# Layer norm's reciprocal standard deviation: square root on ScalarE and reciprocal on VectorE, or add and power on GpSimd

## The chip, the cores and the metric

The kernel runs on one core of one Trainium2 chip. The metric is the device time of one execution in microseconds (us). One step of the norm, done 30 times on small tiles (128 partitions x 2), is moved from ScalarE and VectorE to GpSimd; the big work, 7424 matmuls, is the same in both kernels.

Engine names in the profile: PE is TensorE's matmul, PEld its weight load, DVE is VectorE, ACT is ScalarE, POOL is GpSimd. SBUF is the on-chip memory that tiles lie in; PSUM is the one that matmuls write to. A hole is a stretch in which TensorE is idle. The granted clock of TensorE is given as a share of full speed.

## The reference, cut to what matters

Two layers. Each is a norm, a sliding-window attention (`_A_ref`, 8 dilated positions), a norm, and a gated feed-forward (`_B_ref`).

```python
def _layernorm(x, axis=-1, eps=1e-5):
    m = jnp.mean(x, axis=axis, keepdims=True)
    v = jnp.var(x, axis=axis, keepdims=True)
    return (x - m) / jnp.sqrt(v + eps)

def _B_ref(x, w1, w3, w2):
    gate = jnp.einsum("bsd,df->bsf", x, w1)
    up = jnp.einsum("bsd,df->bsf", x, w3)
    h = _silu(gate) * up
    return jnp.einsum("bsf,fd->bsd", h, w2)

x = x + _A_ref(_layernorm(x), A_wqkv, A_wo)     # x is 1 x 2048 x 1024
x = x + _B_ref(_layernorm(x), B_w1, B_w3, B_w2) # 1024 -> 3584 -> 1024
# ... and the same two lines again
```

## The kernel before: what the change and the argument touch

The program is a list of eight feed-forward units, 0 to 7: two layers times four chunks of 512 tokens. Beneath the matmuls of a unit VectorE works on the attention of the *next* unit: multiplications `pr` (scores) and `tm` (values), each with two operands in SBUF, and their sums. At two places of the unit, at tile 19 and tile 27 of 28, half a norm of the next unit is inserted. That half runs with the same raised priority as the products `hT` that TensorE waits for.

```python
def ln_half(key, c, r):                      # half a norm: two token tiles
    with hp():                               # raised priority
        ...
        for i in range(2):
            n = c * TPC + 2 * r + i
            for hh in range(2):
                nc.vector.bn_stats(st[:, i, hh, :], x_sb[:, n, hh * 512:(hh + 1) * 512])
            nc.vector.bn_aggr(mv[:, i, :], st[:, i, :, :])
        nc.scalar.activation(sd[:], mv[:, :, 1], ACTF.Sqrt, bias=epst[:])
        nc.vector.reciprocal(rstd[:], sd[:])
        for i in range(2):
            j = 2 * r + i
            xn = xnp.tile([P, D], BF16, name="xn")
            nc.vector.tensor_scalar(xn[:], x_sb[:, c * TPC + j, :], mv[:, i, 0:1], rstd[:, i:i + 1],
                                    op0=ALU.subtract, op1=ALU.mult)
            nc.sync.dma_start_transpose(out=xnT[:, :, j * P:(j + 1) * P], in_=xn[:])

def b_stage(l, c, inserts):                  # one unit
    for (f0, f1) in fsplits:                 # (0, 16), then (16, 28)
        ... # for each tile f, after what `inserts` has for it:
                pg = ...                     # 8 matmuls: gate
                pu = ...                     # 8 matmuls: up
                with hp():
                    nc.scalar.activation(sg[:], pg[:], ACTF.Silu)
                    nc.vector.tensor_tensor(hT[:, g0 + fi - f0, :], sg[:], pu[:], op=ALU.mult)
        for hh in range(2):
            for j in range(TPC):
                acc = bank("acc")
                for f in range(f0, f1):      # second product; needs hT of all f
                    nc.tensor.matmul(acc[:], lhsT=hT[:, f - f0, j * P:(j + 1) * P], rhs=...,
                                     start=(f == f0), stop=(f == f1 - 1))
                ...                          # x_sb += acc

# in the loop over the units; n and c2 are of the next unit:
ins = {17: [O(l2, n)], 19: [O(l2, n + 1), lambda: ln_half(("B", l2, c2), c2, 0)],
       25: [O(l2, n + 2)], 27: [O(l2, n + 3), lambda: ln_half(("B", l2, c2), c2, 1)]}
```

I call the second product after tiles 0 to 15 "acc A" (128 matmuls) and the one after tiles 16 to 27 "acc B" (96 matmuls). The twelfth matmul of acc B needs the `hT` of tile 27, the last one. "First half" and "second half" are the calls of `ln_half` at tile 19 and tile 27.

## Time and profile before

| | before |
|---|---|
| median of 3 runs, us | 1636.41 (1635.89 to 1637.51) |
| span of the profiled run, us | 1635.4 |
| granted TensorE clock, mean | 0.998 |
| ScalarE table loads | 59 |

The busy table of the page (busy us, share of the span, number of instructions) says which engine is the limit:

```profile
PE 1616.1 (99%) x7472; PEld 800.2 (49%) x7472; DVE 1152.4 (70%) x1961; ACT 340.5 (21%) x530; POOL 1.9 (0%) x12
```

TensorE is busy for all but about 19 us: 5.2 of these are in the first 13.9 us, the start, and 3.5 come after the last matmul. The list of waits of the kernel before (who waited on which line for whom: total us, times, longest us) has nearly all of the rest:

```profile
PEld L327 <- DVE hT L314: 9.0, 8, 2.6
...
PE pg L305 <- DMA xnT<-xn: 4.9, 1, 4.9
PE acc L327 <- DVE hT L314: 4.7, 3, 2.1
```

So the last `hT` of a stage is already late in three of the sixteen acc stages, 4.7 us together. TensorE nowhere waits for ScalarE's square root; VectorE's reciprocal does, five times, 2.5 us in all.

What the change will take away stands among the groups of instructions of ScalarE (count, busy us, mean ns, idle us before them). Line 128 is the square root; 40 more table loads belong to Silu, Exp and the start:

```profile
L128 ACT ACT_TABLE_LOAD x19 | 24.4, 1283 | 1.4 <-DVE mv L125 1.2
L128 ACT ACTIVATE sd<-mv,epst 128x2 f32<-128x2 f32 x30 | 8.7, 295 | 127.8 <-DVE mv L125 127.7
```

A load takes 1283 ns, which is what the Trainium skill, "ScalarE: Activation LUTs", What ACT_TABLE_LOAD costs, states. The page adds a drain of about 1380 ns to each switch; this trace shows none. At 1464 us the square root ends at 1464.69, a load runs from 1464.71 to 1465.99, and Silu starts at 1466.00: 1.31 us from end to start.

Last, the timeline at the end of unit 2 (start us, duration us, engine, line, what, and in brackets the idle time before it and its releaser):

```profile
705.25 21.13 PE L327 MATMUL acc<-w2t,hT 128*128 128x512 bf16 x96
...
705.92 0.20 DVE L125 BATCH_NORM_AGGREGATE mv<-st 128x2 f32<-128x12 f32 x1
706.03 1.17 DVE L228 TENSOR_TENSOR pr<-qT,kT 128x2048 bf16<-128x2048 bf16 x1
706.15 0.29 ACT L128 ACTIVATE sd<-mv,epst 128x2 f32<-128x2 f32 x1 [0.53 <-DVE mv L125]
707.12 0.68 DVE L314 TENSOR_TENSOR hT<-sg,pu 128x512 bf16<-128x512 bf16 x1
707.72 0.15 DVE L129 RECIPROCAL rstd<-sd 128x2 f32<-128x2 f32 x1
...
708.38 0.54 DVE L133 TENSOR_SCALAR xn<-x_sb,mv,rstd 128x1024 bf16<-128x1024 bf16 x1
```

Acc B starts at 705.25 us, and its 96 matmuls run in one piece. VectorE goes from one instruction to the next without a pause: the square root (706.15 to 706.44) hides under `pr`, and the last `hT` ends at 707.80, about when the twelfth matmul needs it.

### The profile page before, as it was taken

To read this page: it belongs to the slowest core of one execution; us is meant where nothing else is said; L and a number is where in the kernel's file an instruction comes from. 1 tells how busy PE (TensorE), PEld (TensorE's weight loads), DVE (VectorE), ACT (ScalarE), POOL (GpSimd) and SP (SyncE) were. 2 spreads that over 40 slices of the span, in tenths; PEclk is the share of its full clock that TensorE was granted. 3 is DMA by queue.
4 is the path that set the end of the run, shared out by engine and by line. 5 is a ranking of instruction groups with operands and counts; after the bars stand their busy time and mean duration, and the time that the engine had idled before them with its cause. 6 is when DMAs were issued, how large, how long until landed. Compare 5 with 4: busy or idle time off the path is not lost.

```text
span 1635.4 us, 18944 instructions
## 1 busy us (share of the span) xinstructions
PE 1616.1 (99%) x7472; PEld 800.2 (49%) x7472; DVE 1152.4 (70%) x1961; ACT 340.5 (21%) x530; POOL 1.9 (0%) x12
## 2 busy tenths in 40 slices
PE   8999899999999999999999999999999999999999
PEld 5666444444444644446444554445544444444444
DVE  4899999999999781897728977299652992332212
ACT  3333311203021320223202232022320211121110
POOL 0000000000000000000000000000000000000000
PEclk9999999999999999999999999999999999999999
DMA  9943746557546774367743686438753574256440
GB/s 297 280 132 102 220 158 195 159 151 209 183 131 180 240 235 150 106 193 245 221 142 104 199 259 200 142 104 249 255 178 119 129 232 155 90 143 205 155 129 26
DMA packets 337113, 286.32 MB, mean 175 GB/s; under 512 B 69632, under 2 KB 319488, under 8 KB 336896
## 3 DMA queue, kind: packets, MB, share of 16 engines
q1 hardware_dynamic: 337024, 285.11, 57.2%
q8 instruction: 58, 0.95, 0.2%
q14 instruction: 31, 0.25, 0.0%
HBM read 239.99 MB, written 29.36 MB: 165 GB/s over the span
## 4 chain that ended last, share of the span: by engine, by line
PE 67%; DVE 29%; issue 3%; DMA 1%; ACT 0%; DVEq 0%; ACTq 0%
PE acc L327 21%; PE pg L305 15%; PE pu L309 15%; PE ps L202 13%; DVE pr L228 5%; DVE tm L273 4%; PE po L283 3%; DVE hT L314 3%; DVE tm L174 3%; DVE pr L174 2%; DVE x_sb L287 1%; DVE st L124 1%; DVE tm L175 1%; DVE pr L175 1%; DVE L L235 1%
## 5 line engine op out<-in xcount | busy, mean ns | idle before, releaser
L305 PE MATMUL pg<-xnT,w1t 128*128 128x512 bf16 x1792 | 424.7, 380 | 4.9 <-DMA xnT<-xn 4.9
L309 PE MATMUL pu<-xnT,w3t 128*128 128x512 bf16 x1792 | 423.7, 379 | 0.0
L327 PE MATMUL acc<-w2t,hT 128*128 128x512 bf16 x1792 | 390.8, 379 | 5.1 <-DVE hT L314 4.7
L202 PE MATMUL ps<-xnT,wqkv 128*128 128x512 bf16 x1536 | 334.3, 380 | 1.8 <-ACT xnT L163 1.1
L313 ACT ACTIVATE sg<-pg 128x512 bf16<-128x512 f32 x224 | 133.4, 597 | 843.2 <-PE pg L305 831.4
L314 DVE TENSOR_TENSOR hT<-sg,pu 128x512 bf16<-128x512 bf16 x224 | 152.1, 679 | 212.2 <-PE pu L309 210.7
L305 PEld LDWEIGHTS <-w1t 128*128 128x128 bf16 x1792 | 175.5, 98 | 217.0 <-issue 6.6
L327 PEld LDWEIGHTS <-hT 128*128 128x128 bf16 x1792 | 174.8, 98 | 218.5 <-DVE hT L314 9.0
L309 PEld LDWEIGHTS <-w3t 128*128 128x128 bf16 x1792 | 175.5, 98 | 212.0 <-issue 1.0
L202 PEld LDWEIGHTS <-wqkv 128*128 128x128 bf16 x1536 | 220.5, 144 | 114.6 <-issue 3.9
L332 DVE TENSOR_TENSOR x_sb<-x_sb,acc 128x512 bf16<-128x512 bf16 x128 | 87.0, 680 | 162.2 <-PE acc L327 162.2
L228 DVE TENSOR_TENSOR pr<-qT,kT 128x2048 bf16<-128x2048 bf16 x128 | 153.1, 1210 | 51.6 <-issue 32.1
L273 DVE TENSOR_TENSOR tm<-At,vT 128x2048 bf16<-128x2048 bf16 x128 | 151.7, 1213 | 0.3
L204 ACT CAST sgt<-ps 128x512 bf16<-128x512 f32 x192 | 108.7, 588 | 184.6 <-PE ps L202 151.7
L283 PE MATMUL po<-wo,oT 128*128 128x512 bf16 x512 | 115.4, 379 | 0.0
L124 DVE BATCH_NORM_STATS2 st<-x_sb 128x6 f32<-128x512 bf16 x120 | 79.9, 681 | 18.0 <-DMA x_sb<-in_A_x_dram 17.3
L174 DVE TENSOR_TENSOR pr<-pr 128x1024 bf16<-128x1024 bf16 x128 | 85.6, 680 | 0.0
L174 DVE TENSOR_TENSOR tm<-tm 128x1024 bf16<-128x1024 bf16 x128 | 84.4, 681 | 0.0
L283 PEld LDWEIGHTS <-oT 128*128 128x128 bf16 x512 | 50.0, 98 | 60.4
L287 DVE TENSOR_TENSOR x_sb<-x_sb,po 128x512 bf16<-128x512 bf16 x64 | 43.2, 677 | 15.4 <-PE po L283 15.4
L175 DVE TENSOR_TENSOR pr<-pr 128x512 bf16<-128x512 bf16 x128 | 51.8, 415 | 0.2
L175 DVE TENSOR_TENSOR tm<-tm 128x512 bf16<-128x512 bf16 x128 | 50.3, 415 | 0.1
(169 smaller groups left out, 428.7 us busy)
## 6 DMA issues: line engine op xcount, KB each, us to landing
w1t<-in_B_w_dram SPq DMA_DIRECT2D x56, 1024.0 KB, 5.4
w3t<-in_B_w_dram SPq DMA_DIRECT2D x56, 1024.0 KB, 7.2
w2t<-in_B_w_dram SPq DMA_DIRECT2D x48, 1024.0 KB, 5.4
wqkv<-in_A_wqkv_dram SPq DMA_DIRECT2D x28, 1024.0 KB, 6.6
w2t<-in_B_w_dram SPq DMA_DIRECT2D x16, 512.0 KB, 5.1
qkv_d_0_158<-sgt SPq DMA_DIRECT2D x16, 256.0 KB, 5.3
qkv_d_1_159<-sgt SPq DMA_DIRECT2D x16, 256.0 KB, 4.4
qT<-qkv_d_0_158 SPq DMA_DIRECT2D x8, 512.0 KB, 4.0
```

The costliest lines, as they stand in the source:

```text
L174: nc.vector.tensor_tensor(buf[:, 0:4, :], buf[:, 0:4, :], buf[:, 4:8, :], op=ALU.add)
L175: nc.vector.tensor_tensor(buf[:, 0:2, :], buf[:, 0:2, :], buf[:, 2:4, :], op=ALU.add)
L202: nc.tensor.matmul(ps[:], lhsT=ws[kk // KH][:, kk % KH, t::KT], rhs=xnT[:, kk, :], start=(kk == 0), stop=(kk == KT - 1))
L204: nc.scalar.copy(sgt[:, t - t0, :], ps[:])
L228: nc.vector.tensor_tensor(pr[:], qT[:], kT[:, :, k0:k0 + TCH], op=ALU.mult)
L273: nc.vector.tensor_tensor(tm[:], At[:], win, op=ALU.mult)
L283: nc.tensor.matmul(ps[:], lhsT=oT[:, t, j * P:(j + 1) * P], rhs=wo[:, t, hh * 512:(hh + 1) * 512], start=(t == 0), stop=(t == KT - 1))
L305: nc.tensor.matmul(pg[:], lhsT=w1t[:, kk, fi * P:(fi + 1) * P], rhs=xnT[:, kk, :], start=(kk == 0), stop=(kk == KT - 1))
L309: nc.tensor.matmul(pu[:], lhsT=w3t[:, kk, fi * P:(fi + 1) * P], rhs=xnT[:, kk, :], start=(kk == 0), stop=(kk == KT - 1))
L313: nc.scalar.activation(sg[:], pg[:], ACTF.Silu)
L314: nc.vector.tensor_tensor(hT[:, g0 + fi - f0, :], sg[:], pu[:], op=ALU.mult)
L327: nc.tensor.matmul(acc[:], lhsT=hT[:, f - f0, j * P:(j + 1) * P], rhs=w2ts[(f - f0) // 8][:, (f - f0) % 8, :], start=(f == f0), stop=(f == ...
```

## The change

ScalarE spends 24.4 us on loading the square root's tables, and more on loading those of Silu and Exp again, because the three alternate. The intent is to have no square root there at all: GpSimd, which is idle, adds epsilon and raises the sum to the power of minus one half, and VectorE is rid of the reciprocal.

```diff
+    mhalf = const.tile([P, 2], FP32, name="mhalf")
+    nc.gpsimd.memset(mhalf[:], -0.5)
 ...
             sd = small.tile([P, 2], FP32, name="sd")
             rstd = small.tile([P, 2], FP32, name="rstd")
-            nc.scalar.activation(sd[:], mv[:, :, 1], ACTF.Sqrt, bias=epst[:])
-            nc.vector.reciprocal(rstd[:], sd[:])
+            nc.gpsimd.tensor_tensor(sd[:], mv[:, :, 1], epst[:].to_broadcast([P, 2]), op=ALU.add)
+            nc.gpsimd.tensor_tensor(rstd[:], sd[:], mhalf[:], op=ALU.pow)
```

## The prediction

> **What bounds the kernel.** TensorE. The busy table has PE at 1616.1 of 1635.4 us, clock granted at 0.998. In the timeline eight 128x512 matmuls take 1.73 us, so the 7424 large matmuls need about 1603 us (estimate). The list of waits and the timeline leave these holes in PE: the start (13.9 us, a norm routine that the change does not touch), about 6.7 us at 196 to 206 us (first feed-forward stage, waiting for the transposed norm), 2.3, 2.0 and 0.9 us at 261, 345 and 424 us (second product waiting for hT), 0.7 us at 187 us. So at most 12 us (0.8%) could be won.
>
> **What goes.** On ScalarE: 30 square roots (295 ns each, 8.7 us) and their 19 table loads (1283 ns each, 24.4 us). The Trainium skill, "ScalarE: Activation LUTs", What ACT_TABLE_LOAD costs, gives the same 1283 ns. ScalarE is busy 21%; none of the five PE holes was ended by it, the late hT being held by VectorE's queue. On VectorE: 30 reciprocals, 158 ns, 4.7 us of 1152. So nearly all of the saving is off the critical path.
>
> **What comes.** 30 adds and 30 powers of 128x2 on GpSimd, in series with two more hand-overs. The trace has no such instruction; a memset of 128x1 takes 0.10 us, an affine select 0.28. I estimate 0.2 us for an add and 0.5 us for a power, 0.8 to 1.2 us from the statistics to rstd including hand-overs, against 0.57 us in the tight case at 1464 us.
>
> **What moves.** TensorE's order is unchanged. VectorE's is not: the scheduler now puts the apply (xn) ahead of the last hT of a feed-forward stage. Before: aggregate, pr, hT, reciprocal, xn. After, in units 1 to 4 (of 0 to 7): aggregate, pr, xn, hT; in units 0 and 5 two xn. VectorE works in order, so hT now waits for GpSimd. There is no slack there: in unit 1 hT ended at 507.26 us and the twelfth matmul of acc needs it at about 507.25. And the Trainium skill, "SBUF — State Buffer", Who interferes with whom, says a VectorE instruction with two SBUF inputs and a GpSimd instruction reading SBUF exclude each other: the add, released while pr (1.17 us) runs, would start only after pr. No run shows that yet. Then hT is late by xn (0.46) plus 0.8, about 1.3 us, five times, plus half a us more in unit 5: 7 us; unit 0 about +1.4. The hole at 196 to 206 us: as before. VectorE's freed 4.7 us may take 1 us off the holes at 261 and 424.
>
> **Sum.** 1636.4 + 7 + 1.4 - 1 is about 1644 us; 1635 to 1657 should hold it 8 times in 10. Same within 2%: 0.93; slower 0.06; faster 0.01.
>
> **What would show it.** Table loads fall from 59 to 29 and ScalarE's busy time by 47 us, without a shorter span. PE waits "acc <- hT" at five or six stage ends, 1 to 2 us each; VectorE waits about 1 us for rstd before xn. GpSimd's add starting as pr ends shows the port claim; starting within pr refutes it.
>
> **What would make it wrong.** A power that takes 2 to 3 us (then each stage end loses 3 us or more, 1655 to 1660); GpSimd not blocked by pr (then only 0.5 us a unit, about 1639); a VectorE order that shrinks the other holes (then equal or 3 us faster).

## The result, and the profile after

| | before | after |
|---|---|---|
| median, us (4 runs each, same rounds) | 1636.72 | 1660.41 (1658.9 to 1661.61) |
| ratio | | 1.0143, 95% interval 1.0128 to 1.0159 |
| span of the profiled run, us | 1635.4 | 1658.6 |
| granted clock, mean | 0.998 | 0.990 |
| ScalarE busy, us / table loads | 340.5 / 59 | 296.6 / 29 |

Here and below a ratio is the mean time of one kernel's fast runs over the mean of the other's fast runs of the same rounds, so it is not quite the ratio of the medians.

The kernel became 1.4% slower. That is within 2%, as expected, but above the upper end of the range (1657). The busy table after:

```profile
PE 1626.2 (98%) x7472; PEld 803.1 (48%) x7472; DVE 1154.0 (70%) x1931; ACT 296.6 (18%) x470; POOL 40.2 (2%) x73
```

ScalarE lost 43.9 us of work. TensorE, with the same number of matmuls, was busy 10 us longer, and 13 us more of its time lies idle. The waits after:

```profile
DVE xn L135 <- POOL rstd L131: 21.0, 27, 1.1
PE acc L329 <- DVE hT L316: 18.4, 8, 2.9
...
PE pg L307 <- DMA xnT<-xn: 4.3, 1, 4.3
```

VectorE now waits 27 times for GpSimd, and TensorE's wait for `hT` rose from 4.7 to 18.4 us. The new groups of GpSimd:

```profile
L131 POOL TENSOR_TENSOR rstd<-sd,mhalf 128x2 f32<-128x2 f32 x30 | 21.9, 734 | 2.0
L130 POOL TENSOR_TENSOR sd<-mv,epst 128x2 f32<-128x2 f32 x30 | 16.4, 551 | 1445.6 <-DVE mv L127 1445.6
```

The add's mean of 551 ns mixes mainly two kinds, 0.20 us and about 1.06 us. All twelve of 1.06 us ran beside a `pr` or `tm`, and each ended 0.05 or 0.06 us after it. The timeline has one of each: the first line is from the first norm of the feed-forward, beside a VectorE instruction with one input in PSUM; the others are from unit 2, first half (676 to 679 us) and second half (712 us on).

```profile
187.52 0.20 POOL L130 TENSOR_TENSOR sd<-mv,epst 128x2 f32<-128x2 f32 x1 [120.67 <-DVE mv L127]
...
676.16 1.17 DVE L275 TENSOR_TENSOR tm<-At,vT 128x2048 bf16<-128x2048 bf16 x1
676.33 1.06 POOL L130 TENSOR_TENSOR sd<-mv,epst 128x2 f32<-128x2 f32 x1 [139.70 <-DVE mv L127]
677.47 0.69 POOL L131 TENSOR_TENSOR rstd<-sd,mhalf 128x2 f32<-128x2 f32 x1
678.19 1.00 DVE L135 TENSOR_SCALAR xn<-x_sb,mv,rstd 128x1024 bf16<-128x1024 bf16 x2 [0.86 <-POOL rstd L131]
...
712.23 2.54 PE L329 MATMUL acc<-w2t,hT 128*128 128x512 bf16 x11
713.75 0.20 DVE L127 BATCH_NORM_AGGREGATE mv<-st 128x2 f32<-128x12 f32 x1
713.87 1.17 DVE L230 TENSOR_TENSOR pr<-qT,kT 128x2048 bf16<-128x2048 bf16 x1
714.03 1.06 POOL L130 TENSOR_TENSOR sd<-mv,epst 128x2 f32<-128x2 f32 x1 [35.87 <-DVE mv L127]
715.17 0.69 POOL L131 TENSOR_TENSOR rstd<-sd,mhalf 128x2 f32<-128x2 f32 x1
715.89 0.55 DVE L135 TENSOR_SCALAR xn<-x_sb,mv,rstd 128x1024 bf16<-128x1024 bf16 x1 [0.86 <-POOL rstd L131]
716.35 0.68 DVE L316 TENSOR_TENSOR hT<-sg,pu 128x512 bf16<-128x512 bf16 x1
717.09 20.21 PE L329 MATMUL acc<-w2t,hT 128*128 128x512 bf16 x85 [2.32 <-DVE hT L316]
```

Read it in four steps.

1. The add is on record from 714.03 but ends at 715.09, 0.05 us after `pr` (713.87 to 715.04). Elsewhere it takes 0.20 us. Then comes the power, 0.69 us, and VectorE, which works in order, stands still for 0.86 us.
2. `xn` now stands ahead of `hT` in VectorE's order, 0.46 us from its start to the start of `hT`.
3. The same 0.86 us were lost once already, in the first half at 678 us. VectorE never has a pause afterwards in which to make them good: the aggregate of the second half comes 1.52 us after the start of acc B (713.75 - 712.23), where it came 0.67 us after it before (705.92 - 705.25). The difference is 0.85 us.
4. The sum, 0.86 + 0.86 + 0.46 = 2.18 us, is the size of the hole, 2.32 us. After the hole 85 matmuls take 20.21 us. In kernels with a short hole the same 85 take 18.52 us (below).

For step 4, look at the hole of unit 1 (510.0 to 512.79 us) in windows. The columns are window, us, then busy us of PE, PEld, DVE, ACT, POOL with the number of instructions, then the granted clock, the DMA share and GB/s:

```profile
512.50:514.00 1.50, 1.21 (x3) 0.43 (x4) 1.50 (x4) 0.00 (x0) 0.00 (x0) 0.50 0.48 92
514.00:516.00 2.00, 2.00 (x6) 0.73 (x5) 2.00 (x5) 0.00 (x0) 0.00 (x0) 0.53 0.90 152
516.00:518.00 2.00, 2.00 (x11) 0.90 (x10) 2.00 (x4) 0.00 (x0) 0.00 (x0) 1.00 1.02 381
```

The clock is 0.50 for about three microseconds after the hole, and a matmul takes twice as long in it: 6 began in the second window, 11 in the third. PE reads as fully busy in both, so the busy row does not show it.

The ledger, from the timeline of TensorE, each stage from its start to the start of the next, in us:

| stage | before | after | difference |
|---|---|---|---|
| acc A of unit 0 | 29.91 | 31.81 | +1.90 |
| acc B of unit 0 | 22.75 | 23.77 | +1.02 |
| acc A of unit 1 | 28.55 | 28.30 | -0.25 |
| acc B of units 1, 2, 3, 4, 5 | 20.96 each | 25.20, 24.90, 24.91, 24.91, 25.36 | +20.48 |
| sum | | | +23.15 |

The spans differ by 23.2 us, so this is all of it. Acc B of unit 6, where no norm follows, is 20.72 us in both.

### The profile page after: what moved, and what is told of

Read it like the earlier page. It is cut to its first block, busy times and chain, and to the rows that moved or that the text cites. A ratio compares the mean times of both kernels' runs of the same rounds, so it can differ in the third digit from the quotient of the medians.

```text
span 1658.6 us, 18939 instructions
## 1 busy us (share of the span) xinstructions
PE 1626.2 (98%) x7472; PEld 803.1 (48%) x7472; DVE 1154.0 (70%) x1931; ACT 296.6 (18%) x470; POOL 40.2 (2%) x73
## 4 chain that ended last, share of the span: by engine, by line
PE 67%; DVE 27%; issue 3%; POOL 1%; DMA 1%; ACT 0%; DVEq 0%; SPq 0%; ACTq 0%
PE acc L329 21%; PE pg L307 15%; PE pu L311 15%; PE ps L204 12%; DVE tm L275 4%; DVE pr L230 4%; PE po L285 3%; DVE hT L316 3%; DVE pr L176 2%; DVE tm L176 2%; DVE st L126 1%; DVE x_sb L289 1%; DVE pr L177 1%; DVE tm L177 1%; DVE oT L178 1%
## 5 line engine op out<-in xcount | busy, mean ns | idle before, releaser
L329 PE MATMUL acc<-w2t,hT 128*128 128x512 bf16 x1792 | 400.6, 386 | 18.4 <-DVE hT L316 18.4
L126 DVE BATCH_NORM_STATS2 st<-x_sb 128x6 f32<-128x512 bf16 x120 | 80.0, 682 | 16.4 <-DMA x_sb<-in_A_x_dram 15.6
L130 POOL TENSOR_TENSOR sd<-mv,epst 128x2 f32<-128x2 f32 x30 | 16.4, 551 | 1445.6 <-DVE mv L127 1445.6
```

## The experiments

Theory: the loss is (a) the late `hT`, made of the wait in both halves and of the new order, and (b) the slower clock after a hole of about 2 us or more. Rivals: that what ScalarE does, or no longer does, matters; that GpSimd's power is simply slow; that the matmuls after the hole are slow because something else in the memory disturbs them; that the first half's wait is absorbed before the stage ends.

| run | median, us | before, same rounds | ratio (95%) |
|---|---|---|---|
| e1_no_tables | 1640.0 | 1636.71 | 1.0022 (1.0008 to 1.0035) |
| e2_ht_first | 1644.84 | 1636.71 | 1.0051 (1.0037 to 1.0064) |
| e3_zero_matmuls | 1653.82 | 1636.71 | 1.0105 (1.0091 to 1.0119) |
| e4_scalar_apply | 1641.62 | 1636.71 | 1.0028 (1.0014 to 1.0041) |
| e5_add_on_scalar | 1653.02 | 1637.52 | 1.0094 (1.008 to 1.0108) |
| e6_first_half_scalar | 1648.09 | 1637.52 | 1.0066 (1.0052 to 1.008) |
| e7_power_twice | 1676.79 | 1637.52 | 1.0239 (1.0224 to 1.0255) |
| e8_selected_apply | 1643.9 | 1637.52 | 1.0041 (1.0029 to 1.0054) |
| e9_before_apply_q | 1638.77 | 1636.97 | 1.001 (0.9996 to 1.0024) |
| e10_before_apply_all | 1637.91 | 1636.97 | 1.0006 (0.9993 to 1.0018) |
| e11_pool_first_ffn | 1640.42 | 1636.51 | 1.0023 (1.0011 to 1.0036) |
| e12_pool_first_ffn_all | 1639.92 | 1636.51 | 1.002 (1.0006 to 1.0034) |

All but the first gave correct results. In these rounds the kernel before has nine runs, each variant four or five. The kernel after was not run again in them: what a variant won is counted from its 1660.41 us, and the medians of the kernel before differ by 1.0 us between rounds.

### The table loads alone (e1)

The kernel before, with a function in place of the square root that needs no table load between its neighbours, as the count below shows. The result is wrong (relative error 16); the instructions are as many as before.

```diff
-            nc.scalar.activation(sd[:], mv[:, :, 1], ACTF.Sqrt, bias=epst[:])
+            nc.scalar.activation(sd[:], mv[:, :, 1], ACTF.Identity, bias=epst[:])
```

> The kernel before with Identity in place of Sqrt in the norm (result wrong on purpose): the 19 table loads in front of the square roots and about ten reloads after them go, GpSimd does nothing, the last hT stays ahead of xn. My theory: the table loads were off the critical path, so the time stays within 3 us of before (1634 to 1640 us), with ScalarE's busy time some 38 us less. Rival (the table loads were worth something that the change gave back elsewhere): 5 us or more below before, 1631 us or less.

Table loads fell from 59 to 29 and ScalarE's busy time from 340.5 to 302.2 us; the time did not fall. The span grew by 3.4 us, nearly all of it before acc B of unit 2 (which starts at 708.50 in place of 705.25). Acc B of unit 0, where the scheduler now put two `xn` ahead of the last `hT`, alone took 3.2 us longer:

```profile
349.75 20.21 PE L327 MATMUL acc<-w2t,hT 128*128 128x512 bf16 x85 [3.37 <-DVE hT L314]
```

Before, this hole was 1.86 us. Outside this stage the gains and losses come to 0.2 us. So the loads that the change removes won nothing here, and the loss isn't bound to GpSimd alone: a hole of 3.37 us costs 20.21 us for 85 matmuls in a kernel that does no arithmetic on GpSimd after the start.

### The order of VectorE (e2)

The kernel after, with the last `hT` of each stage raised in priority, so that the scheduler puts it ahead of `xn` again. GpSimd's two instructions stay.

```diff
-                    with hp():
+                    with tc.high_priority(offset=BOOST * (2 if g0 + fi == f1 - 1 else 1)):
                         sg = sgp.tile([P, CH], BF16, name="sg")
```

> The changed kernel with a higher priority for the last silu and hT of each half of a stage, which puts hT ahead of xn again; GpSimd does the same work. My theory: the TensorE hole at the end of units 1 to 5 falls from 2.3 to 2.8 us to about 1.1 us (what stays is the 0.86 us that VectorE lost at its first wait for GpSimd in the same stage, and the 0.24 us of before), and the slow matmuls after it go: about 17 us come back, 1643 us (1639 to 1648). Rival (GpSimd's latency as such, or some cost outside the stage ends, makes the time): stays at 1655 us or more.

Unit 2 in its timeline:

```profile
711.55 0.71 DVE L316 TENSOR_TENSOR hT<-sg,pu 128x512 bf16<-128x512 bf16 x1
...
712.32 18.52 PE L329 MATMUL acc<-w2t,hT 128*128 128x512 bf16 x85 [0.93 <-DVE hT L316]
```

The hole went from 2.32 to 0.93 us: `hT` no longer waits for the second half's power nor for `xn` (0.86 + 0.46 = 1.32 us). What is left is the first half's 0.86 us, and the 85 matmuls are at full speed. Acc B of units 2 to 5 took 21.82 us each in place of 24.9 to 25.4. This run won back 15.6 of the 23.7 us by the medians (1660.41 - 1644.84), though it lost some in unit 0, where acc A grew to 33.30 us from the 31.81 of the kernel after.

### The clock alone (e3)

The kernel after, with eight matmuls with a weight of zeros just before the matmul that waits, in units 1 to 5. They add nothing to `acc`, cost TensorE 1.91 us that it would have idled, and leave `hT` as late as it is.

```diff
+    zt = const.tile([P, 64], BF16, name="zt")
+    nc.gpsimd.memset(zt[:], 0.0)
 ...
                     for f in range(f0, f1):
+                        if hh == 0 and j == 0 and lastsplit and f == f1 - 1 and 1 <= l * NCH + c <= 5:
+                            for _ in range(8):
+                                nc.tensor.matmul(acc[0:64, :], lhsT=zt[:], rhs=w2ts[0][:, 0, :], start=False, stop=False)
```

> The changed kernel with eight 64-column matmuls of a zero tile into acc just before the matmul that waits for the last hT, in units 1 to 5 only (result unchanged). They need 1.73 us and fall into the hole of 2.3 to 2.8 us. My theory: TensorE is then never idle for more than about 1 us there, the matmuls after the hole run at 216 ns from the first one, and 1.5 to 1.7 us per hole come back, 8 us in all: 1652 us (1649 to 1655). Rival (the matmuls after the hole are slow for another reason, such as contention with the transposes or VectorE): 1659 us or more.

Unit 2:

```profile
712.70 2.54 PE L334 MATMUL acc<-w2t,hT 128*128 128x512 bf16 x11
715.17 1.91 PE L333 MATMUL acc<-w2t,zt 128*64 128x512 bf16 x8
717.57 18.52 PE L334 MATMUL acc<-w2t,hT 128*128 128x512 bf16 x85 [0.48 <-DVE hT L318]
```

The twelfth matmul starts 4.87 us after the first (717.57 - 712.70), as in the kernel after (717.09 - 712.23 = 4.86): `hT` is just as late. But the 85 matmuls take 18.52 in place of 20.21 us. So 1.69 us of this unit's loss is the clock's answer to the hole, and no other disturbance that stays with the late `hT`. Acc B of units 1 to 4 took 23.22 us each, of unit 5 23.68, together 8.7 us less than in the kernel after. By the medians the run gained 6.6 us; 1.9 us were lost again in acc A of unit 1, where a hole of 2.43 us came up (30.23 us in place of 28.30).

### The port claim, and the power held in place of the add (e5)

The kernel after, with the add on ScalarE, in a function that needs no table load (29 loads, as in the kernel after); the power stays on GpSimd.

```diff
-            nc.gpsimd.tensor_tensor(sd[:], mv[:, :, 1], epst[:].to_broadcast([P, 2]), op=ALU.add)
+            nc.scalar.activation(sd[:], mv[:, :, 1], ACTF.Identity, bias=epst[:])
```

> The changed kernel with the add of epsilon moved to ScalarE (Identity with a bias, in any table, so no table load); only the power stays on GpSimd, VectorE's order unchanged. GpSimd now asks for SBUF with the power some 0.4 us after the aggregate, while VectorE's pr or tm (two SBUF inputs, 1.17 us) runs. Theory (they exclude each other): the power is recorded longer than the 0.69 us of a free one, 1.3 us or so, VectorE still waits 0.5 to 0.8 us before xn, holes of units 1 to 4 are 1.7 to 2.2 us, time 1648 to 1658 us. Rival (no exclusion; the add's 1.06 us had another cause): power at 0.69 us, wait 0.2 us or less, holes below 1 us, 1641 to 1645 us.

```profile
713.43 1.17 DVE L230 TENSOR_TENSOR pr<-qT,kT 128x2048 bf16<-128x2048 bf16 x1
713.60 0.29 ACT L130 ACTIVATE sd<-mv,epst 128x2 f32<-128x2 f32 x1 [2.47 <-DVE mv L127]
713.98 1.17 POOL L131 TENSOR_TENSOR rstd<-sd,mhalf 128x2 f32<-128x2 f32 x1 [36.26 <-ACT sd L130]
715.18 0.55 DVE L135 TENSOR_SCALAR xn<-x_sb,mv,rstd 128x1024 bf16<-128x1024 bf16 x1 [0.58 <-POOL rstd L131]
```

ScalarE's instruction ran under `pr` in its usual 0.29 us. The power, which takes 0.69 us when `pr` is over, now takes 1.17 us and ends 0.55 us after `pr` (715.15 - 714.60). The same GpSimd instruction is longer or shorter by what VectorE runs beside it, which is the rule of the Trainium skill, "SBUF — State Buffer", Who interferes with whom: a VectorE instruction with two SBUF inputs and a GpSimd instruction that reads SBUF contend. The trace agrees in kind; in amount, 0.14 us of the power (0.69 - 0.55) and 0.15 us of the add (0.20 - 0.05) did run while `pr` held it off. Beside `hT`, which has one input in PSUM, the power keeps its 0.69 us (at 374.15 us in the kernel after). The longest case is in e4, below, beside some 11 us of VectorE instructions with both inputs in SBUF; the power ended 0.55 us after the last of them:

```profile
66.30 11.73 POOL L133 TENSOR_TENSOR rstd<-sd,mhalf 128x2 f32<-128x2 f32 x1 [11.20 <-ACT xn L140]
```

So hiding the power under `pr` mostly fails: the wait in the second half is 0.58 us in place of 0.86. The holes of units 2 to 4 are 1.78 us, that of unit 1 is 2.16, and the 85 matmuls after them stayed at 18.52 us; unit 5's of 2.24 us was slow (20.21).

### The first half (e6)

The kernel after, with the old square root and reciprocal in the feed-forward norms' first half only. Both versions have the second half on GpSimd.

```diff
+            if key[0] == 'B' and r == 0:
+                nc.scalar.activation(sd[:], mv[:, :, 1], ACTF.Sqrt, bias=epst[:])
+                nc.vector.reciprocal(rstd[:], sd[:])
+            else:
                 nc.gpsimd.tensor_tensor(sd[:], mv[:, :, 1], epst[:].to_broadcast([P, 2]), op=ALU.add)
                 nc.gpsimd.tensor_tensor(rstd[:], sd[:], mhalf[:], op=ALU.pow)
```

> The changed kernel with only the first half of each feed-forward norm back to square root on ScalarE and reciprocal on VectorE; the second half, at the stage end, and all other norms stay on GpSimd. Theory (VectorE is saturated from the first half to the stage end, so both 0.86 us waits end in the same hole): holes of units 1 to 4 fall from 2.33 to about 1.5 us, of unit 5 to 1.9, the slow matmuls after them go, 1647 us (1644 to 1650). Rival (only the wait next to the stage end counts): holes stay at 2.3 us and the time at 1658 to 1660 us.

```profile
709.73 0.20 DVE L127 BATCH_NORM_AGGREGATE mv<-st 128x2 f32<-128x12 f32 x1
...
711.88 0.55 DVE L139 TENSOR_SCALAR xn<-x_sb,mv,rstd 128x1024 bf16<-128x1024 bf16 x1 [0.86 <-POOL rstd L135]
...
713.08 18.52 PE L333 MATMUL acc<-w2t,hT 128*128 128x512 bf16 x83 [1.47 <-DVE hT L320]
```

Acc B starts at 709.07 us here, so the aggregate comes 0.66 us after it, as in the kernel before. The second half still waits its 0.86 us, and the hole is 1.47 us: 0.85 less than in the kernel after. The wait in the first half, some 37 us earlier, is carried whole to the stage's end. (Here 83 matmuls are on record; about 2% of the records are missing from this trace. The time from first to last can still be compared.)

With e2 the hole closes: it takes away 1.39 us, e6 0.85 us, together 2.24 of 2.32 us. The two were not run together.

### The power twice (e7)

The kernel after, with a power of one before the power of minus one half.

```diff
+            nc.gpsimd.tensor_tensor(s1[:], sd[:], mone[:], op=ALU.pow)   # mone holds 1.0
-            nc.gpsimd.tensor_tensor(rstd[:], sd[:], mhalf[:], op=ALU.pow)
+            nc.gpsimd.tensor_tensor(rstd[:], s1[:], mhalf[:], op=ALU.pow)
```

> The changed kernel with one more power on GpSimd (exponent one, result unchanged) between add and power: 0.69 us and a hand-over more in series. Theory: each wait grows from 0.86 to 1.6 us and each hole of units 1 to 4 by twice that growth, from 2.33 to 3.9 us, unit 5 to 4.3; the time grows by about 9 us to 1670 us (1666 to 1676). Rival (GpSimd's time is hidden and the order alone makes the loss): stays within 2 us of 1660.

Units 2 and 3:

```profile
727.92 0.55 DVE L139 TENSOR_SCALAR xn<-x_sb,mv,rstd 128x1024 bf16<-128x1024 bf16 x1 [1.63 <-POOL rstd L135]
...
934.95 21.18 PE L333 MATMUL acc<-w2t,hT 128*128 128x512 bf16 x83 [3.88 <-DVE hT L320]
```

A second power costs a half 0.77 us (1.63 - 0.86), and the hole 1.55 us (3.87 in unit 2 against 2.32): twice 0.77. That is the carrying of the first half once more, from the other side. In unit 3 the slow stretch also grew: 21.18 us for the rest of the stage in place of 20.21. Acc B of the five units took 135.45 us in place of 125.28, so 2.0 us a unit for a power of 0.69 us. The rest of the rise is mainly in unit 0 (acc A 32.96, acc B 27.49 us) and at the hole before the first feed-forward, which grew from 4.27 to 6.83 us. By the medians the run lost 16.4 us where 9 had been expected; the expectation covered the five late holes alone.

### The apply on ScalarE (e4, e8)

If `xn` leaves VectorE, VectorE doesn't wait for GpSimd at all. The kernel after, with `xn` as an activation with scale and bias; the bias, minus mean times rstd, is two more GpSimd multiplications. In e4 for all norms of `ln_half`, in e8 for those of the feed-forward except the first one's.

```diff
+            mr = small.tile([P, 2], FP32, name="mr")
+            nc.gpsimd.tensor_tensor(mr[:], mv[:, :, 0], rstd[:], op=ALU.mult)
+            nc.gpsimd.tensor_tensor(mr[:], mr[:], mone[:], op=ALU.mult)      # mone holds -1.0
 ...
-                nc.vector.tensor_scalar(xn[:], x_sb[:, c * TPC + j, :], mv[:, i, 0:1], rstd[:, i:i + 1],
-                                        op0=ALU.subtract, op1=ALU.mult)
+                nc.scalar.activation(xn[:], x_sb[:, c * TPC + j, :], ACTF.Identity, bias=mr[:, i:i + 1], scale=rstd[:, i:i + 1])
```

> The changed kernel with xn made on ScalarE (Identity with scale rstd and bias minus mean times rstd; two more small GpSimd multiplications), so that VectorE never waits for GpSimd and loses 60 xn of 0.54 us. My theory: no wait of VectorE for GpSimd, no hole at the end of units 1 to 5, other holes of before equal or smaller: 1628 to 1637 us, so not slower than the kernel before. If the 30 power operations cost the time by themselves wherever they are consumed, it stays near 1660 us.

> A version meant to be fast: the changed kernel with xn on ScalarE for the feed-forward norms of units 1 to 7 only (as in the run with all applies on ScalarE, whose units 1 to 5 had holes of 0.5 us), and on VectorE for the attention norms and the first feed-forward norm, where that run's hole had grown from 4.3 to 7.5 us. Theory: holes of units 1 to 5 at 0.5 us, the one at 200 us back at about 4.3 us: 1634 to 1639 us, equal to the kernel before or 2 us faster. Rival: the ScalarE applies delay the silu elsewhere: 1640 us or more.

In both the hole of units 1 to 5 is 0.52 or 0.53 us and the matmuls after it are at 18.52 us: the 20 us of the late stages are all but gone. GpSimd's add is as slow as ever (1.06 us in unit 2 of e4), it just isn't waited for by the queue that `hT` stands in. What stays of the loss is early. In e4 the hole before the first feed-forward grew to 7.54 us and acc B of unit 0 had one of 2.75 us with slow matmuls behind it; e8 mended the first (4.51 us) and had 3.42 us in unit 0, again with slow matmuls, and 2.47 in acc A. They come to 1641.62 and 1643.9 us: better than the kernel after, not as good as the kernel before, and both above what was expected.

### Trying for a version that beats both (e9 to e12)

The kernel before, with its square root, and `xn` on ScalarE: for the attention norms of the first layer (e9) or for all but the first feed-forward norm (e10).

```diff
+            on_act = key[0] == "Q" and key[1] == 0        # e9; in e10: key != ("B", 0, 0)
+            if on_act:
+                mr = small.tile([P, 2], FP32, name="mr")
+                nc.vector.scalar_tensor_tensor(mr[:], mv[:, :, 0], -1.0, rstd[:], op0=ALU.mult, op1=ALU.mult)
 ...            # where on_act: xn by nc.scalar.activation, as in e4
```

> No GpSimd at all: the kernel before (square root on ScalarE, reciprocal on VectorE) with xn of the first attention layer's norms 1 to 3 on ScalarE, to take some 4 us of work from VectorE before 200 us, where it is saturated. Theory: VectorE reaches unit 0 earlier, the holes of before at 261, 345 and 424 us (2.3, 2.0, 0.9 us) shrink, 1631 to 1636 us. Rival: those holes come from the order of instructions in front of the hT and not from the backlog: 1636 us or more.

> The kernel before with xn on ScalarE for every norm except the first attention norm (left as it is) and the first feed-forward norm. Theory: as the run with the attention norms alone, and in units 1 to 5 VectorE has 0.5 to 1 us less to do per half before the last hT, so the 0.24 us lost there goes too: 1630 to 1636 us. Rival: the applies sit in ScalarE's queue in front of a silu and make a last hT late: 1638 us or more.

The late holes shrank, from 2.11 + 1.86 + 0.75 us to 1.64 + 1.24 (e9) and 1.26 + 1.01 (e10). But the hole before the first feed-forward, 4.86 us before, grew:

```profile
204.45 3.57 PE L312 MATMUL pg<-xnT,w1t 128*128 128x512 bf16 x8 [8.77 <-DMA xnT<-xn]
```

VectorE now had a copy of 1.23 us just ahead of that norm's reciprocal, and a transpose of 2.31 us between the reciprocal and its `xn`. Both intervals include 1. Next, the same two kernels with GpSimd's add and power for that one norm alone, where the kernel after had a shorter hole (4.27 us):

```diff
+            if key == ("B", 0, 0):
+                nc.gpsimd.tensor_tensor(sd[:], mv[:, :, 1], epst[:].to_broadcast([P, 2]), op=ALU.add)
+                nc.gpsimd.tensor_tensor(rstd[:], sd[:], mhalf[:], op=ALU.pow)
+            else:
                 nc.scalar.activation(sd[:], mv[:, :, 1], ACTF.Sqrt, bias=epst[:])
                 nc.vector.reciprocal(rstd[:], sd[:])
```

> A version meant to beat both: the kernel with the attention norms' applies on ScalarE, and GpSimd's add and power for one norm only, the first feed-forward norm, where square root and Exp alternate on ScalarE and the hole before the first feed-forward matmul had grown to 8.8 us (VectorE's queue had put a copy and a transpose of 3.5 us before the reciprocal). Theory: that hole falls to 4 to 5 us as in the changed kernel, the others stay small: 1632 to 1635 us, faster than before by 2 to 5 us. Rival: the hole stays above 7 us, or a new one opens at 261 us: 1637 us or more.

> The same with the applies of all norms but the first attention norm and the first feed-forward norm on ScalarE. Theory: 1631 to 1635 us. Rival: 1637 us or more.

That hole fell to 5.42 and 5.82 us, and holes of 3.62 and 3.38 us came up in acc A of unit 0, which e9 and e10 had not (in e12 also one of 2.90 us in acc B). Both are 0.2% slower than the kernel before. None of the four reached the time expected of it. Each edit reorders VectorE's queue in unit 0 and the hole comes back at another stage; why the scheduler picks each order was not looked into. No version that I ran beats the kernel before.

A power on VectorE itself, fused with the add in one instruction or apart, was to take GpSimd out of the chain. It did not build, nor did add and power fused on GpSimd; I didn't find out why.

## Why the prediction was right or wrong

**Right.** TensorE bounds the kernel and ScalarE's work is off the critical path: 30 table loads fewer (59 to 29, as predicted), 43.9 us less busy (predicted 47), and no gain from it, which e1 shows alone. The scheduler's new order of VectorE (`xn` ahead of the last `hT`) is in the trace. GpSimd's add was held by `pr` and ended as `pr` did; the free add takes 0.20 us as estimated, the power 0.69 (estimated 0.5), the wait of VectorE is 0.86 us (predicted 0.8). The hole at about 200 us stayed (4.86 to 4.27 us).

**Wrong: "hT is late by xn (0.46) plus 0.8, about 1.3 us, five times ... 7 us".** The five units lost 20.5 us, 3.9 to 4.4 each. The 1.3 us is right for what it covers: e2 takes just that away and the hole shrinks by 1.39 us. Two terms are missing from the sum.

- *The first half's wait.* I had costed the wait only at the norm beside the stage's end. The same wait happens at tile 19, and VectorE, although busy 70% of the span, is full from there to the end of the stage. So another 0.86 us arrives at `hT` undiminished. The aggregate's distance from the start of acc B shows it (1.52 against 0.67 us), e6 takes it away (hole 1.47 us), and e7 doubles up on both halves (0.77 us longer wait, 1.55 us longer hole).
- *The clock.* The prediction has no term for it: it took a hole to cost its own length. Holes of 2.3 to 2.8 us also had TensorE at a clock of 0.50 for about 3 us, which cost 1.5 to 1.7 us more; e3 takes this away and leaves the late `hT`. The Trainium skill, "TensorE: Matmul & The Clock Gate", Why this matters for your kernels, advises no idle gaps above about 3 us; these were shorter. Holes of the predicted 1.3 us would probably have been safe, as those of 1.39 (e2) and 1.47 us (e6) were: it is the first missing term that made the holes long enough for the second.

For unit 2 the sum is 0.86 + 0.86 + 0.46 + 1.69 = 3.87 us, of 3.94 measured (24.90 - 20.96).

**Wrong in size: "unit 0 about +1.4".** It was +1.90 in acc A and +1.02 in acc B; of the first, 1.41 us are slow matmuls (25.97 us for 113, against 24.56).

**"VectorE's freed 4.7 us may take 1 us off the holes at 261 and 424":** the one at 424 us went from 0.75 to 0.50, the one at 261 rose from 2.11 to 2.47.

**The alternative that fits by accident.** The prediction named a power of 2 to 3 us as what would give 1655 to 1660 us. The total came out at its upper end by luck: the power takes 0.69 us. A total that matches does not confirm its cause; the timeline of one stage refutes this one at a glance.

**When a hole slows the clock.** The length of the hole alone does not decide. The clock dropped after holes of 1.97 (e3, at 185.7 us, where it fell 1.2 us after the hole), 2.09 (e3, acc A of unit 0), 2.24 (e5), 2.32 (after) and 3.37 us (e1), and not after 2.11 (before), 2.16 (e5), 2.43 (e3), 2.88 (after, acc B of unit 0) or 3.38 us (e12). The Trainium skill, "TensorE: Matmul & The Clock Gate", Part 1, describes a window of fixed length that runs freely, and the traces agree. The clock falls in units 1 to 5 of the kernel after at 512.47, 717.27, 922.07, 1126.87 and 1331.67 us. These are always 204.80 us apart, which is 60 times 3.413, while the ends of the holes are 204.30 to 204.93 us apart. Between the first and the last matmul, slow stretches last 3.41 us or two or three times that, and in each of the fourteen traces all changes of the clock fit one grid of that period, to 0.004 us. Read the kernel after in windows of this grid, first at the hole of 2.88 us and then at that of 2.32 us (same columns as above):

```profile
345.20:348.62 3.42, 2.22 (x11) 0.78 (x8) 2.59 (x5) 0.00 (x0) 1.75 (x2) 1.00 0.82 282
348.62:352.03 3.41, 1.73 (x8) 0.80 (x9) 3.39 (x6) 0.00 (x0) 0.00 (x0) 1.00 0.48 90
352.03:355.44 3.41, 3.41 (x17) 1.56 (x16) 3.41 (x9) 0.00 (x0) 0.00 (x0) 1.00 0.95 223
...
713.86:717.27 3.41, 1.09 (x6) 0.31 (x4) 2.55 (x5) 0.00 (x0) 1.75 (x2) 1.00 1.13 311
717.27:720.68 3.41, 3.41 (x9) 1.22 (x8) 3.41 (x9) 0.00 (x0) 0.00 (x0) 0.50 0.80 169
720.68:724.10 3.42, 3.42 (x17) 1.57 (x16) 3.21 (x6) 0.00 (x0) 0.00 (x0) 1.00 0.94 292
```

The longer hole is cut by the grid into 1.2 and 1.7 us, and the next window stays fast; the shorter one lies whole in one window, and the next window is slow. Over all traces, past the start, a fast window with 1.88 us of idle PE or less was never followed by a slow one, one with 2.06 us or more always was, and of six between 1.95 and 2.04 us three were. So whether a hole of 2 to 3.4 us costs the extra 1.5 to 1.7 us depends on where it falls on the grid. That all five of the kernel after did is in part luck, and is known of its profiled execution only.

**What stays open.** I did not follow up why unit 1's hole is 0.47 us longer than unit 2's (2.79 against 2.32). The holes of the timeline are given as recorded; from start to start they are some 0.17 us longer, as the record of the last matmul before a hole ends later than the usual distance between two.

## What to carry to other kernels

An engine with 30% idle time in the whole span can have none in the stretch that counts: look from the place of the change to the next wait on the limiting engine, and add up every delay that the change puts into that in-order queue, not only the last one. When the sum gives TensorE a hole of about 2 us or more, allow for a slow clock after it, here 1.5 to 1.7 us for each of the late holes. And before moving small work to an idle engine, ask who stands in line behind its result: the same GpSimd work, with the waiting instruction on another engine (e4), left only 0.3% to lose.

## What the Trainium skill lacked or had wrong

- "TensorE: Matmul & The Clock Gate", Part 1 and Why this matters for your kernels: the window of about 3.4 us that runs freely agrees with the traces (3.41 us). But half speed is tied to a whole window of idleness, and gaps up to about 3 us are taken as safe. Here about 2 us of idle PE within one window were enough (never at 1.88 us or less, always at 2.06 or more), and holes of 1.97 and 2.09 us (e3), 2.24 (e5) and 2.32 us (after) were followed by half speed. A hole of 3.38 us (e12) that the grid cut in two was not.
- "SBUF — State Buffer", Who interferes with whom: the rule held (the add 1.06 us beside `pr`, 0.20 us beside an instruction with a PSUM input; a power of 11.73 us in e4). What the page lacks is which part of a GpSimd instruction is held off: the add ended 0.05 us after `pr`, of 0.20 us alone, and the power 0.55 us after it, of 0.69, so about 0.15 us of each was not.
- "GPSIMD Engine Reference": no duration for a power, nor for an add this small. Measured at 128x2 in float32: add 0.20 us, power 0.69 us, and 0.77 us for one more power in a chain.
- "ScalarE: Activation LUTs", What ACT_TABLE_LOAD costs: the 1283 ns agree. A drain of about 1380 ns more is said to come with every switch, 2.66 us in all; in the kernel before, 21 of its loads left at most 1.5 us, and as little as 1.31 us, between the end of the instruction before and the start of the one after.
